# A new global order and engine choice for the operations ahead of the token mix, in a kernel of a gated long convolution followed by a gMLP mixer

## The chip, the cores and the metric

The kernel runs on one core of a Trainium2 chip. The core has five engines that each work through their own list of instructions in order: TensorE (PE, matrix products, with its weight loads listed apart as PEld), VectorE (DVE), ScalarE (ACT), GpSimd (POOL) and SyncE (SP, which issues most of the DMA transfers). They wait for one another by semaphores. The metric is device time in microseconds (us), the median of several executions. The profile is taken from one execution; its span runs from the first to the last instruction.

## The reference

Sequence length 2048 (16 tiles of 128 tokens), width 640 (5 blocks u of 128 channels), bf16. Cut to what matters:

```python
mod = (silu(c) @ w_mod).reshape(1, 6, 1, 640)
sa, ca, ga, sb, cb, gb = mod[:, 0], ..., mod[:, 5]

h = layernorm(q) * (1 + ca) + sa
k_shift = sum over t of k_pad[:, t:t + S] * shift_k[:, 3 - t]      # short convolution, 4 taps
kv = k_shift * v
y = irfft(rfft(kv, 2 S) * rfft(ssm_k, 2 S))[:S] + kv * ssm_D       # long convolution
x = q + ga * (h * y)

h = layernorm(x) * (1 + cb) + sb
z = gelu(h @ w_in)                                                # 640 -> 1728
z1, z2 = z[:, :864], layernorm(z[:, 864:])
g = w_sp @ z2 + b_sp[:, None]                                     # token mix, 2048 x 2048
return x + gb * ((z1 * g) @ w_out)
```

## The kernel before

The kernel is written as a plan. Each step of the computation is recorded as one of 1444 operations with the engines that may run it and the operations on which it depends. Nothing is scheduled by rule: a text constant named `ORDER` lists all operations, each as a letter for its engine (P for PE, D for DVE, A for ACT, G for POOL, S for SP) and its number. One loop hands them out in this order:

```python
        order = [(x[0], int(x[1:])) for x in ORDER.split()]
        assert sorted(i for _, i in order) == list(range(len(self.ops)))
        done = set()
        for e, i in order:
            o = self.ops[i]
            assert e in o["eng"] and done.issuperset(o["deps"]), (e, i)
            ...
            o["fn"](engines[e])
            done.add(i)
```

So `ORDER` fixes two things: the sequence on every engine, and which engine does an operation that has a choice. An engine that waits holds up everything behind it on its own list. Tiles lie in a fixed number of buffers per tag (four PSUM tags, `s1`, `sm`, `pu` and `pz`, serve everything up to the mix), and a new tile in a tag waits for the last reader of the tile that held the buffer.

The stages, with the names of operations that the text below uses (line numbers are of the kernel before):

- **Head and front** (0 to about 129 us). The long convolution is done as a Fourier transform by matrix products. Per block u of channels: the short convolution on PE and its product with v on DVE (L616), the first transform stage with its copies out of PSUM (`s1c`, 1024 columns in one copy or 512 in one, tile `s`, L278), the forward stage into `pu`, the product with the filter's spectrum (`prod`, L495, DVE alone, 1.2 us each, tiles `T` and `Tf` from `pu` and `KH`), for half of them a sum of halves (`csum`, L509, POOL or DVE), the inverse stage into `pz` and its copy out (`zc`, L278, tile `Z` from `pz`), then the last stage (`yl`, matrix products with `Ebd`) and the product with h (`ym`, L770). `zk` are the copies that regroup between stages. Beside it run the first layernorm (`xn`, L697 to L699, and `ghm`, L753, which applies 1 + ca and sa) and the sum x = q + ga * (...) (`res`, L808, with the statistics `ln2`, L814).
- **Second layernorm and zz** (about 125 to 191 us). The 16 tiles of tokens are taken in four groups of four. Per tile the aggregate, the power on POOL (L218 and L219), and the normalised tile (`zx`, L957 on ACT, L959 on POOL, L961 on DVE). The first group is transposed on PE in pieces (`hfl`, L972) and modulated by `hmod` (L983 on ACT, L985 on DVE). The other groups are transposed by one DMA each (L1003) and modulated in place, by channel block, by `hmod2` (five per group, L1009 on ACT, L1011 on DVE or POOL). Then come 64 groups of five matmuls of 432 columns (`zz`), each followed by a gelu on ACT (L1034) and, for the half that is normalised, a statistic (`stz`, L1040) and an aggregate (L1044). When four tiles have theirs, POOL makes the power (`rstdz`), DVE the offset (`nmrz`, L1049), and DVE or ACT normalise (`zn`, L1055 and L1057).
- **Token mix** (from 190.6 us). The product w_sp @ z2 is computed by seven products of halves (`m1` to `m7`), in the manner of Strassen's scheme, of sums of w_sp's blocks (`S1` to `S4`, L1101) and of z2's (`T1` to `T4`, L1111), at L1126. Then the output product.
- **Fill.** Four `fill` operations, each a few matmuls of the identity whose result nobody reads; the one that matters here, of two matmuls of 512 columns, stands ahead of the first zz.

## Time and profile before

| what | value |
|---|---|
| time, median of three runs | 305.8 us (305.66 to 307.07) |
| span of the profiled execution | 303.8 us |
| mean granted clock of TensorE in the span | 0.989 |
| instructions in the span | 7152 |
| bytes moved by DMA | 41.57 MB, 137 GB/s on average |

The profile gives no device time of the profiled execution itself; the 2.0 us between its span and the median are what lies around the span. PE does 2827 matmuls. A window view gives, for any stretch of the span, how long each engine was busy in it (with the number of instructions), the clock that TensorE was granted (1.00 is full speed), and the DMA engines' share. A group view gives one row per kind of instruction: line, engine, operation, output and input tiles with shapes, count, then busy time and mean duration in ns, then the idle time ahead of it. A timeline row is a start, a length, and what ran; neighbours of one kind are merged into one row with their count. The chain of waits is read backwards in time from the end: each piece is what the next one waited for.

### The profile page before, as it was taken

To read this page: it belongs to the slowest core of one execution; us is meant where nothing else is said; L and a number is where in the kernel's file an instruction comes from. 1 tells how busy PE (TensorE), PEld (TensorE's weight loads), DVE (VectorE), ACT (ScalarE), POOL (GpSimd) and SP (SyncE) were. 2 spreads that over 40 slices of the span, in tenths; PEclk is the share of its full clock that TensorE was granted. 3 is DMA by queue.
4 is the path that set the end of the run, shared out by engine and by line. 5 is a ranking of instruction groups with operands and counts; after the bars stand their busy time and mean duration, and the time that the engine had idled before them with its cause. 6 is when DMAs were issued, how large, how long until landed. Compare 5 with 4: busy or idle time off the path is not lost.

```text
span 303.8 us, 7152 instructions
## 1 busy us (share of the span) xinstructions
PE 293.1 (96%) x2827; PEld 207.0 (68%) x2827; DVE 260.4 (86%) x527; ACT 164.0 (54%) x299; POOL 186.8 (61%) x213
## 2 busy tenths in 40 slices
PE   6899999999999999799999999999999999999996
PEld 2788999999989988645555555555555555665664
DVE  8899999999989999989595988988678798886794
ACT  5989999998888865446665779500111102111110
POOL 5463788839769997577537342099531863476771
PEclk9999999999999999869999999999999999999999
DMA  7999869792397978005997900057654446452433
GB/s 143 270 242 271 194 177 282 134 223 39 77 186 163 287 122 276 2 2 105 157 234 154 197 0 4 0 117 150 132 133 90 102 112 141 102 84 73 91 83 121
DMA packets 117155, 41.57 MB, mean 137 GB/s; under 512 B 102557, under 2 KB 117122, under 8 KB 117122
## 3 DMA queue, kind: packets, MB, share of 16 engines
q1 hardware_dynamic: 116968, 41.08, 62.0%
q8 instruction: 22, 0.36, 0.5%
q14 instruction: 11, 0.09, 0.1%
q10 hardware_dynamic: 154, 0.05, 0.1%
HBM read 16.60 MB, written 2.63 MB: 63 GB/s over the span
## 4 chain that ended last, share of the span: by engine, by line
PE 80%; DVE 8%; SPq 5%; DMA 3%; issue 2%; POOL 1%; ACT 0%; DVEq 0%; POOLq 0%
PE ps L1126 23%; PE pu L275 19%; PE pz L275 17%; PE po L1335 5%; PE sm L275 5%; PE s L275 4%; SPq L570 3%; DVE Tf L495 3%; PE po L1348 3%; DMA ZT<-in_A_v_dram 3%; PE pz L1126 2%; PE pu L1126 1%; DVE Z L616 1%; SPq L585 1%; DVE ot L1394 1%
## 5 line engine op out<-in xcount | busy, mean ns | idle before, releaser
L275 PEld LDWEIGHTS <-Z 128*128 128x128 bf16 x320 | 32.0, 100 | 28.8 <-issue 3.0
L275 PE MATMUL pu<-X,M 128*128 128x128 bf16 (+1 forms) x480 | 45.6, 237 | 0.9 <-DVE Tf L495 0.7
L509 POOL TENSOR_TENSOR W<-Tf 128x256 bf16<-128x256 f32 x42 | 30.7, 745 | 15.0 <-DVE Tf L495 9.0
L275 PEld LDWEIGHTS <-M 128*128 128x128 bf16 x480 | 36.7, 98 | 4.2 <-issue 1.6
L1126 PEld LDWEIGHTS <-S 128*128 128x128 bf16 x256 | 25.0, 98 | 20.8
L275 PE MATMUL pu<-big,Z 128*128 128x432 bf16 x160 | 34.6, 360 | 0.0
L278 ACT CAST X<-s 128x1024 bf16<-128x1024 f32 x32 | 32.7, 1021 | 3.3 <-PE s L275 3.2
L275 PE MATMUL pz<-big,Z 128*128 128x432 bf16 x160 | 33.0, 349 | 0.0
L495 DVE TENSOR_TENSOR Tf<-pu,KH 128x1024 f32<-128x1024 f32 x25 | 30.3, 1215 | 1.2 <-ACT Z L278 0.5
L1132 ACT COPY m<-ps 128x432 f32<-128x432 f32 x7 | 3.6, 521 | 49.8 <-PE ps L1126 41.0
L1126 PEld LDWEIGHTS <-wT 128*128 128x128 bf16 x192 | 18.8, 98 | 15.3
L278 ACT CAST Z<-pz 128x512 bf16<-128x512 f32 x40 | 23.5, 596 | 4.9 <-PE pz L275 4.7
L275 PEld LDWEIGHTS <-G 128*128 128x128 bf16 x330 | 24.6, 98 | 1.8 <-issue 0.4
L278 ACT CAST KH<-pu 128x512 bf16<-128x512 f32 x40 | 23.1, 592 | 3.8 <-PE pu L275 3.4
L1126 PE MATMUL ps<-X,wT 128*128 128x432 bf16 x112 | 22.7, 346 | 0.0
L1126 PE MATMUL ps<-X,S 128*128 128x432 bf16 x112 | 22.6, 346 | 0.0
L1040 DVE BATCH_NORM_STATS2 stz<-X 128x6 f32<-128x432 bf16 x32 | 18.1, 588 | 5.0 <-ACT X L1034 4.9
L1126 PE MATMUL ps<-T,S 128*128 128x432 bf16 x112 | 22.2, 346 | 0.0
L275 PE MATMUL sm<-dg,big 128*128 128x128 bf16 x320 | 20.7, 219 | 1.1 <-DVE Z L616 1.0
L275 PEld LDWEIGHTS <-big 128*128 128x128 bf16 x320 | 18.9, 98 | 2.0 <-issue 1.6
L495 DVE TENSOR_TENSOR T<-pu,KH 128x1024 bf16<-128x1024 f32 x15 | 18.2, 1215 | 1.9 <-PE pu L275 1.8
L275 PEld LDWEIGHTS <-X 128*128 128x128 bf16 x288 | 17.8, 98 | 2.2 <-POOL X L433 0.7
(223 smaller groups left out, 666.7 us busy)
## 6 DMA issues: line engine op xcount, KB each, us to landing
wm<-in_w_mod_dram SPq DMA_DIRECT2D x6, 800.0 KB, 4.9
xt<-in_A_q_dram SPq DMA_DIRECT2D x4, 640.0 KB, 5.6
out_dram<-ot SPq DMA_DIRECT2D x15, 160.0 KB, 1.9
big<-in_B_w_in_dram SPq DMA_DIRECT2D x2, 1080.0 KB, 7.8
X<-in_A_ssm_k_dram SPq DMA_DIRECT2D x4, 512.0 KB, 6.2
ZT<-in_A_v_dram SPq DMA_DIRECT2D x1, 1024.0 KB, 7.6
big<-in_A_v_dram SPq DMA_DIRECT2D x1, 1024.0 KB, 7.8
w_o<-in_B_w_out_dram SPq DMA_DIRECT2D x6, 160.0 KB, 3.5
```

Source lines behind the costliest of these rows:

```text
L275: nc.tensor.matmul(o, lhsT=w, rhs=x, start=start, stop=stop)
L278: (e.copy if e is nc.scalar else e.tensor_copy)(dst, src)
L495: e.tensor_tensor(T_[:], (tl[pu] if src is None else tl[src])[:, :, :, None, :].to_broadcast(shape), tl[KH][:, :, None, :, :].to_broadcast ...
L509: e.tensor_tensor(tl[W][:, :, o, :], T_[:, :, 0, o, :], T_[:, :, 1, 1 - o, :], op=ALU.add if o else ALU.subtract)
L570: e.dma_start_transpose(k_of(u)[:, KPAD + h * m:KPAD + (h + 1) * m], A_k[0, h * m:(h + 1) * m, u * DU:(u + 1) * DU])
L585: e.dma_start(v_of(0, ns.start, NT // n) if u0 == 0 else tl[name][:], v_nat[:, ns, ds])
L616: e.tensor_tensor(dst, tl[ps][:].rearrange("p n (c g) -> p n c g", g=8), v_of(u, i * SCH, SCH).rearrange("p n (c g) -> p n c g", g=8), op= ...
L1040: op("D", "stz", lambda e, i=i, n=n, fc=fc: e.bn_stats(out=stz[:, n, fc, :], in_=tl[z2][:, i, fc * FC:(fc + 1) * FC]), r=[(z2, (i, fc))], ...
L1126: nc.tensor.matmul(ps[:, :FC], lhsT=lhs[:, s_, :], rhs=rhs(s_), start=(s_ == 0 and not more), stop=(s_ == HT - 1), skip_group_check=more)
L1132: e.copy(part[p, m][:], part[p, BANK[m]][:, :FC])
L1335: nc.tensor.matmul(ps[:, :HS], lhsT=w(k), rhs=x(k), start=start and k == 0, stop=stop and k == n - 1, skip_group_check=True)
L1348: e.matmul(po[t, i][:, :hi - lo], lhsT=uTs[t][:fsz[ft], ft, :], rhs=T["w_o"][:fsz[ft], ft, lo:hi], start=(ft == 0), stop=(ft == NFT - 1))
```

## The change

Only the constant `ORDER` differs. The first 1105 entries are put in another sequence, 107 operations are given to another engine, and the last 339 entries, from the middle of the token mix on, are the same as before. No operation is added or removed, so every engine's total changes only by what it takes over. The new constant has two more lines of text, so a line of code L985 in the kernel before is L987 in the changed one.

```diff
@@ ORDER (before: lines 48 to 111, after: lines 48 to 113) @@
-G5 D18 A1 S83 G0 G110 S2 P7 S23 G109 G6 D13 A4 D14 G25 A16 D15 D111 P1041 D10 S26 D112 P8 A38 D17 D113 A11 G89 D130
-A115 D136 P1044 S24 P153 S84 S91 A154 P156 P39 D131 P41 A158 A133 A132 S27 P1043 G90 D118 G134 D40 A137 D119 S3 A114
...
+D109 A4 D0 P1043 A1 G5 S23 P7 A10 A38 D13 D18 G110 D111 D118 D130 G15 G112 D119 A120 P1044 D131 A133 S83 D14 A16 P1041
+S2 G6 P8 A121 A11 A132 G25 P39 D136 A137 D113 A115 G17 D89 P153 A154 P156 A155 D124 D125 A127 A126 S84 S26 D40 D19
...
```

Of the operations that changed engine ahead of the first `hmod`, these go to DVE: from ACT five `zc`, five `s1c` and three or four single copies, from POOL eight `ghm`, three `csum`, two `res`, one `xn` and some small ones of the head. These leave DVE: ten `ghm`, five `csum`, two `xn` and a `res` for POOL, two `s1c` and three `zk` for ACT. On SP the loads keep their order but for one early pair.

Three places show it in rows. The first is on DVE, in the middle of the front. Before, around products of blocks 1 and 2 (tiles `T` and `Tf` out of `pu`; `gh` rows at L753 are `ghm`, rows at L770 `ym`):

```order
L616 TENSOR_TENSOR Z_1628<-sm_1788,big_1103 128x4x16x8
L495 TENSOR_TENSOR T_1876<-pu_1853,KH_1654 128x1024
L495 TENSOR_TENSOR Tf_1900<-pu_1879,KH_1619 128x1024
L753 TENSOR_TENSOR gh_95<-gh_95,gsa_bf_102 128x4x128
L753 TENSOR_TENSOR gh_95<-gh_95,gca1_bf_101 128x4x128 x2
L753 TENSOR_TENSOR gh_95<-gh_95,gsa_bf_102 128x4x128
L616 TENSOR_TENSOR Z_1628<-sm_1903,big_1103 128x4x16x8
L753 TENSOR_TENSOR gh_95<-gh_95,gca1_bf_101 128x4x128
L770 TENSOR_TENSOR gh_95<-gh_95,sm_1838 128x16x8x4
```

And in the changed kernel, around the products of the same stretch:

```order
L497 TENSOR_TENSOR Tf_1745<-pu_1738,KH_1434 128x1024
L497 TENSOR_TENSOR T_1764<-pu_1757,KH_1536 128x1024
L280 CAST Z_1346<-pz_1771 128x32x16
L280 CAST Z_1802<-pz_1803 128x32x16
L497 TENSOR_TENSOR T_1831<-pu_1824,KH_1602 128x1024
L280 CAST Z_1802<-pz_1833 128x32x16
L497 TENSOR_TENSOR Tf_1874<-pu_1867,KH_1657 128x1024
L772 TENSOR_TENSOR gh_95<-gh_95,sm_1748 128x16x8x4
L810 TENSOR_TENSOR xt_68<-xt_68,gh_95 128x4x128
```

Three copies `zc` (CAST of `Z` out of `pz`), which ACT made before, stand between four products, and the `ghm` that stood there have gone elsewhere.

The second is the start of zz. On PE, ahead of the first zz (`pu` out of `big` and `Z`), before:

```order
L972 MATMUL sm_2949<-ident_73,Z_2935 128x128
L275 LDWEIGHTS ident_73
L275 MATMUL s1_2969<-ident_73 128x512
L275 LDWEIGHTS ident_73
L275 MATMUL s1_2969<-ident_73 128x512
L275 LDWEIGHTS Z_2954
L275 MATMUL pu_2981<-big_2374,Z_2954 128x432
```

And now, at the end of the same transposes (`sm` out of the identity and `Z`; the rows `sm` out of `Ebd` are a `yl`, whose 32 matmuls reach up to the first zz):

```order
L974 MATMUL sm_2926<-ident_73,Z_2874 128x128
L974 LDWEIGHTS Z_2874
L974 MATMUL sm_2926<-ident_73,Z_2874 128x128
L277 LDWEIGHTS X_2716
L277 MATMUL sm_2935<-Ebd_100,X_2716 128x4x4
L277 LDWEIGHTS X_2716
L277 MATMUL sm_2935<-Ebd_100,X_2716 128x4x4
```

The fill (`s1` out of the identity) no longer stands there: it is now eight operations of PE's list ahead of zz, before the transposes. One `yl` stands between the transposes and zz instead. On DVE, the modulation of the second group of tiles (`hmod2`, in place on `Z`), before:

```order
L814 BN_STATS st2_72<-xt_68 128x6
L1011 TENSOR_SCALAR Z_3091<-Z_3091,cb1_col_70,sb_col_71 128x4x128
L814 BN_STATS st2_72<-xt_68 128x6
L1011 TENSOR_SCALAR Z_3091<-Z_3091,cb1_col_70,sb_col_71 128x4x128
L814 BN_STATS st2_72<-xt_68 128x6
L943 BN_AGGR mv2_82<-st2_72 128x2
L1040 BN_STATS stz_85<-X1_2980 128x6
L947 SCALAR_TENSOR_TENSOR nmr2_84<-mv2_82,rstd2_83 128x4
```

And now:

```order
L1042 BN_STATS stz_85<-X1_2997 128x6
L1013 TENSOR_SCALAR Z_3073<-Z_3073,cb1_col_70,sb_col_71 128x4x128
L945 BN_AGGR mv2_82<-st2_72 128x2
L1013 TENSOR_SCALAR Z_3073<-Z_3073,cb1_col_70,sb_col_71 128x4x128
L1042 BN_STATS stz_85<-X1_2997 128x6
L1046 BN_AGGR mvz_86<-stz_85 128x2
L1013 TENSOR_SCALAR Z_3073<-Z_3073,cb1_col_70,sb_col_71 128x4x128 x3
L816 BN_STATS st2_72<-xt_68 128x6 x6
```

Before, two of the group's five were DVE's, two POOL's and one ACT's; now all five are DVE's, with a statistic of zz (`stz`) ahead of them, and one more and two aggregates between them.

The third is on DVE at the fourth group of tiles. Before:

```order
L1040 BN_STATS stz_85<-X1_3207 128x6 x2
L1044 BN_AGGR mvz_86<-stz_85 128x2
L1040 BN_STATS stz_85<-X1_3378 128x6 x2
L1044 BN_AGGR mvz_86<-stz_85 128x2
L1011 TENSOR_SCALAR Z_3418<-Z_3418,cb1_col_70,sb_col_71 128x4x128 x2
L1040 BN_STATS stz_85<-X1_3378 128x6
L1011 TENSOR_SCALAR Z_3418<-Z_3418,cb1_col_70,sb_col_71 128x4x128
L1040 BN_STATS stz_85<-X1_3207 128x6
```

And now:

```order
L1042 BN_STATS stz_85<-X1_3332 128x6
L1013 TENSOR_SCALAR Z_3431<-Z_3431,cb1_col_70,sb_col_71 128x4x128
L1046 BN_AGGR mvz_86<-stz_85 128x2
L1042 BN_STATS stz_85<-X1_3194 128x6
L1046 BN_AGGR mvz_86<-stz_85 128x2
L1013 TENSOR_SCALAR Z_3431<-Z_3431,cb1_col_70,sb_col_71 128x4x128
L1046 BN_AGGR mvz_86<-stz_85 128x2
L1042 BN_STATS stz_85<-X1_3332 128x6
L1013 TENSOR_SCALAR Z_3431<-Z_3431,cb1_col_70,sb_col_71 128x4x128
```

Before, the first two of DVE's three modulations stood together; now a statistic and two aggregates stand between them, and the last one still stands behind a statistic of its own. The other two of the five were POOL's; now they are one POOL's and one ACT's.

At the end of zz one zz group moves from ahead of the products to behind `m4`, and `m6` becomes the third product.

## The prediction

> **What bounds the kernel now.** I read the profile from the whole to the place: first the busy times and the chain that ended last, then the span cut into stages, then the waits inside the stage that the change rearranges.

> ```profile
> PE 293.1 (96%) x2827; PEld 207.0 (68%) x2827; DVE 260.4 (86%) x527; ACT 164.0 (54%) x299; POOL 186.8 (61%) x213
> PE 80%; DVE 8%; SPq 5%; DMA 3%; issue 2%; POOL 1%; ACT 0%; DVEq 0%; POOLq 0%
> ```

> TensorE (PE) is busy for 96% of the span and carries 80% of the chain. No matmul is added or removed, so the change can only win or lose PE's idle time, 303.8 - 293.1 = 10.7 us, and time in which PE runs at a lower clock. Where both lie is seen by stage (columns: window, its length, then busy time of PE, weight load, DVE, ACT, POOL, then granted clock, DMA share, GB/s):

> ```profile
> 0.00:24.40 24.40, 20.75 (x237) 16.44 (x238) 21.09 (x64) 20.22 (x44) 13.24 (x35) 1.00 1.08 214
> 24.40:60.00 35.60, 35.26 (x548) 33.21 (x545) 33.71 (x61) 34.60 (x66) 25.02 (x34) 1.00 0.90 218
> 60.00:100.00 40.00, 39.73 (x569) 36.86 (x568) 37.90 (x57) 34.49 (x53) 29.82 (x34) 1.00 0.69 138
> 100.00:128.69 28.69, 25.24 (x490) 23.54 (x487) 27.07 (x52) 18.13 (x32) 23.31 (x27) 0.97 0.62 173
> 128.69:190.77 62.08, 62.08 (x333) 32.90 (x334) 51.21 (x149) 41.28 (x77) 32.27 (x36) 0.96 0.53 104
> 190.77:303.80 113.03, 110.06 (x661) 64.02 (x659) 89.38 (x148) 15.27 (x32) 63.12 (x50) 1.00 0.47 103
> ```

> The first four rows are the convolution with its ends, the fifth the 64 groups zz, the sixth the products and the mix. PE idles 3.65 us up to 24.4, 0.34 and 0.27 in the two middle rows, 3.45 from 100 to 128.69, and not at all in the fifth row, where the clock of 0.96 shows that some of it was slow. So PE bounds from 24.4 to 100 and through zz. But **DVE stands right behind it**: its idle time in the first four rows is 3.31 + 1.89 + 2.10 + 1.62 = 8.92 of 128.69 us, which is 93% busy. What is written on DVE there must fit in 8.92 us.

> The head ends with a transfer that both orders issue at nearly the same place on SP's queue. I therefore count no gain there. The last 3.45 us of PE's idle time are a chain through small operations:

> ```profile
> 125.88 0.88 POOL Z L959
> 126.81 0.69 PE s L972 x6
> 127.58 1.06 DVE Z L985 x3
> 128.69 1.03 PE s L275 x2
> 129.72 1.44 PE pu L275 x4
> ```

> Normalise (Z L959), transpose (hfl, L972), modulate (hmod, L985), then the fill's two matmuls (s L275), then zz (pu L275). This is what the first zz waits for.

> **The change, part by part. DVE up to the start of zz.** Of 107 engine changes those that count are the ones onto and off the fullest vector engine. The prices, grouped by line and shape up to 129 us (last columns: count, busy us, mean ns):

> ```profile
> L509 DVE TENSOR_TENSOR W<-Tf 128x256 bf16<-128x256 f32 x8 | 3.4, 433 | 0.2
> L753 DVE TENSOR_TENSOR gh<-gh,gca_bf 128x512 bf16<-128x512 bf16 x11 | 4.4, 437 | 0.0
> L753 DVE TENSOR_TENSOR gh<-gh,gsa_bf 128x512 bf16<-128x512 bf16 x10 | 5.1, 510 | 0.0
> L278 DVE CAST X<-pu 128x512 bf16<-128x512 f32 x3 | 2.0, 681 | 0.0
> L278 DVE COPY X<-sm 128x1024 bf16<-128x1024 bf16 x6 | 4.0, 668 | 0.1
> L699 DVE TENSOR_SCALAR gh<-xt,mv,rstd 128x640 bf16<-128x640 bf16 x2 | 1.4, 688 | 0.0
> L808 DVE TENSOR_TENSOR xt<-xt,gh 128x512 bf16<-128x512 bf16 x4 | 2.8, 699 | 0.0
> ```

> Onto DVE, ahead of the first hmod, come five copies zc and five copies s1c from ACT, each a 128x512 cast out of PSUM: 10 x 0.681 = 6.8. Eight ghm at the mean of 0.437 and 0.510, 0.47: 3.8. Three csum at 0.433: 1.3. Two res at 0.699: 1.4. One xn at 0.688 and two bf16 copies at 0.668: 2.0. About eight small operations (masks, identity, diagonal) from POOL and ACT, which DVE does not show: at nothing they are 0, at the 0.433 of the nearest row 3.5; as most are narrower, I take 2.3. Sum 17.6. Off DVE go ten ghm, 4.7; five csum, 2.2; two xn, 1.4; one res, 0.7; three copies zk and two s1c, five at about 0.67, 3.4; small ones, taken at 1.1 between 0 and 3. Sum 13.5. **DVE gets about 4.1 us more work**, 2 to 6 with the small ones at their ends. ACT loses about as much, and POOL gains a little under 2; both have over 20 us idle in the four rows, though ACT, 34.60 of 35.60, has only 1.0 in the second.

> What 4.1 us do is decided by the 8.92. If DVE uses 4.1 of them, 46%, PE stays the bound and the front ends when it did: 0. If none can be used, it ends 4.1 later. If DVE keeps up with less waiting than that, what can be won is PE's idle 3.45 before 128.69, and no more. The waits on which it hangs are of two kinds:

> ```profile
> DVE T L495 <- PE pu L275: 1.8, 4, 0.8
> DVE Z L616 <- DMA ZT<-in_A_v_dram: 0.5, 1, 0.5
> DVE Tf L495 <- ACT Z L278: 0.5, 1, 0.5
> ```

> These are DVE's longest waits from 24.4 to 117. Most are a product waiting for its transform, four times for 1.8 in total: time into which an independent copy fits exactly. The wait on ACT's copy (0.5) goes where DVE makes the copy itself. I take the front at **0**, between -3.4 and +4.1. Against it speaks that a DVE copy now stands between two products in the row: the products queued behind it (1.2 us each, and PE's inverse transform behind them) wait for its PSUM tile. With PE nearly gapless, each such wait comes out of PE's time unless another inverse is in hand.

> **The start of zz.** The fill leaves its place between hmod and zz.

> ```profile
> 128.00 1.02 ACT L983 ACTIVATE Z<-sm,sb_col,cb_col 128x256 bf16<-128x256 bf16 x2 [1.33 <-PE sm L972]
> 129.51 3.81 PE L275 MATMUL pu<-big,Z 128*128 128x432 bf16 x10
> ```

> DVE's hmod end at 128.64 and ACT's at 129.02; zz, which began at 129.51, could begin then: -0.49. One yl now stands behind hfl and fills a part of PE's pause ahead of zz. The clock, in windows of 3.4 us, and the matmuls that it slowed:

> ```profile
> 123.60:127.00 3.40, 1.97 (x75) 1.87 (x73) 2.96 (x14) 0.92 (x1) 2.13 (x4) 1.00 0.02 5
> 127.00:130.40 3.40, 2.62 (x15) 1.38 (x13) 3.40 (x10) 1.02 (x2) 2.46 (x4) 0.50 0.00 0
> 130.40:133.80 3.40, 3.40 (x11) 1.37 (x9) 3.40 (x13) 1.35 (x2) 3.28 (x4) 0.50 0.00 0
> ```
> ```profile
> 133.11 2.35 PE L275 MATMUL pz<-big,Z 128*128 128x432 bf16 x10
> 135.30 0.50 PE L972 MATMUL s<-ident,Z 128*128 128x128 bf16 x6
> 144.07 1.99 PE L275 MATMUL pu<-big,Z 128*128 128x432 bf16 x10
> 145.89 1.81 PE L275 MATMUL pz<-big,Z 128*128 128x432 bf16 x9
> ```

> After a window in which PE was busy for 1.97 of 3.40 us the granted clock was 0.50 for two windows. Ten zz matmuls then took 133.11 - 129.51 = 3.60, and the next ten 2.19, where ten at full clock take 145.89 - 144.07 = 1.82: a loss of 1.78 + 0.37 = 2.15 (the next ten begin at 133.11 and end ahead of the transposes at 135.30). The changed order moves the pauses, but its tail chain is as long, so whether the clock falls again I hold at one in two.

> [...]

> [...]

> ```profile
> 138.88 3.00 SPq L1003 DMA_TRANSPOSE Z<-Z  x1
> 143.86 0.43 DVE L1011 TENSOR_SCALAR Z<-Z,cb_col,sb_col 128x512 bf16<-128x512 bf16 x1
> 144.41 0.58 DVE L1011 TENSOR_SCALAR Z<-Z,cb_col,sb_col 128x512 bf16<-128x512 bf16 x1
> 145.11 0.81 ACT L1009 ACTIVATE Z<-Z,sb_col,cb_col 128x512 bf16<-128x512 bf16 x1
> ```

> Its first zz follows the five matmuls at 145.89, at 146.81, 0.89 after the last hmod2 (145.92). With fill and clock gone PE would be there at 146.81 - 0.49 - 2.15 = 144.2. In the new order all five hmod2 stand on DVE, a statistic of zz ahead, and another with two aggregates between: 5 x 0.5 and about 1.3 (two statistics of 0.54, the row further down, and 0.2) are 3.8. They begin between the landing (141.87, or 141.4 with the fill gone) and the old 143.86, so they end between 145.2 and 147.7. Thus the gain is at most 146.81 - 145.2 = 1.6, and it can be a loss of 0.9. I take **-0.8**, near the favourable end, as DVE's wait there was for a gelu that comes earlier too.

> **The rest of zz and the mix.** Group 3's first zz needs a hmod2 that now queues on DVE behind a statistic waiting for its gelu:

> ```profile
> 169.82 0.53 ACT L1034 ACTIVATE G<-pz 128x432 bf16<-128x432 f32 x1 [0.87 <-PE pz L275]
> 170.30 0.39 DVE L1011 TENSOR_SCALAR Z<-Z,cb_col,sb_col 128x512 bf16<-128x512 bf16 x1
> 170.53 1.99 PE L275 MATMUL pu<-big,Z 128*128 128x432 bf16 x10
> 170.61 1.62 DVE L1040 BATCH_NORM_STATS2 stz<-X 128x6 f32<-128x432 bf16 x3
> ```

> Group 3 begins with the second five at 170.53, at 171.44; its last modulation ended at 170.69, 0.75 before. A statistic is 1.62 / 3 = 0.54 and the gelu ahead of it 0.53; if the modulation comes later by both, 1.1, it uses up the 0.75 and PE waits **+0.4**, between 0 and +1. At the end of zz T2 is wanted one product earlier (m6 third). Its second half follows rstdz by nmrz, four zn and one sum, and is read after m6's fourth matmul; I cost it at 0, up to +0.9 (the length of one zz group, which stood ahead of the products and now follows m4). The last 339 operations keep their order: 0.

> Sum: 0 - 0.8 + 0.4 = -0.4. The profiled span is 303.8 and the median 305.8, so 2.0 lie around the span; I keep them: 303.4 + 2.0 = **305.4**.

> **The rivals.** *Faster:* DVE's idle time takes the 4.1 its products end earlier, and PE work that stood before 100 is left to fill the last chain's pause. For it: 1.8 us of its waits are for PE, and PE has 3.45 idle there. Against: DVE would be near 98% busy. At two thirds of the 3.45, -2.3, with z's -0.8 and group 3's +0.4 it is 303.1. It is over 0.5% once PE's 3.45 shrinks by more than 1.1. *Slower:* DVE becomes the bound of the products. Only the idle time of 24.4 to 100, 3.99, is near the new copies; if half of it is usable, 2.0, the front ends 4.1 - 2.0 = 2.1 later and the time is 307.5, and with none 309.5. For it: 93% busy before, and copies that stand ahead of products. It costs over 0.5% as soon as DVE absorbs less than 4.1 - 1.9 = 2.2. *No effect on the front, and z gated:* hmod2 on DVE ends as late as before; the start of zz gives nothing: 306.2. *The clock falls later,* and both windows, 6.8 us, lie wholly in zz: 3.4 lost for the 2.15 of now, so 305.8 + 1.25 - 0.49 + 0.4 = 307.0; for it, the pauses shift against windows that the kernel doesn't set. *The clock does not fall:* the start of zz gives its full 1.6 where the hmod2 allow it, 305.8 - 1.6 + 0.4 = 304.6; for it, the pause that the yl fills; against it, that 1.97 us of matmuls did not keep the clock up before. [...]

> **How the numbers follow.** About 0.5%, 1.5 us, is what can be told from no change here. The forecast, the front at 0, has 0.38 and its own range of 304.3 to 307.3, whatever zz does: of the 0.38, the half gain has 0.17, clock kept 0.10, gated 0.06, clock later 0.05, which lie between 304.6 and 307.0. Faster has 0.36, slower 0.26. The range is 302.4 to 308.4: below it about a quarter of the faster case, above it about two fifths of the slower one.

> **What would show it.** DVE's idle time before the first zz: about 4.8 if the first step is right, about 7 or more where DVE is late. First zz near 129.0. The clock at 0.5 for two windows or for none. Group 1's first zz between 145.5 and 147. A pause under 1 us ahead of group 3. Wrong it would be if PE pauses inside 24.4 to 100, or if the last chain's pause shrinks by more than 1.1.

## The result

The changed kernel takes 327.69 us (median of 4 runs, 324.53 to 329.81) beside 305.73 (305.32 to 307.07): **1.0625** times as long, 95% interval 1.0574 to 1.0675. Two of its four runs fell into the slower state, which the ratio leaves out; without them it is about 325. The forecast was 305.4.

The page of the changed kernel, its busy times and the chain that ended last:

```profile
PE 297.7 (92%) x2827; PEld 207.9 (64%) x2827; DVE 280.5 (87%) x546; ACT 155.9 (48%) x287; POOL 186.4 (57%) x206
PE 49%; DVE 35%; DMA 4%; ACT 4%; POOL 3%; issue 3%; DVEq 0%; POOLq 0%; SPq 0%
```

DVE is busy 20 us longer than before (280.5 for 260.4), and its share of the chain has gone from 8% to 35%: it has taken PE's place as the bound over long stretches. Where the 20.3 us of span (303.8 to 324.1) went is read from windows, cut at the changed kernel's first zz and its first product (columns as in the prediction):

```profile
0.00:24.40 24.40, 20.45 (x224) 15.52 (x225) 22.31 (x63) 19.02 (x39) 15.84 (x35) 1.00 1.02 211
24.40:60.00 35.60, 34.68 (x530) 32.12 (x528) 34.24 (x66) 35.10 (x69) 25.41 (x33) 1.00 1.06 220
60.00:100.00 40.00, 38.89 (x553) 36.41 (x551) 38.35 (x54) 31.22 (x47) 34.26 (x37) 1.00 0.59 124
100.00:133.42 33.42, 28.50 (x537) 26.47 (x536) 31.95 (x59) 17.81 (x33) 22.80 (x28) 0.94 0.64 165
133.42:202.22 68.80, 62.08 (x331) 32.22 (x328) 54.24 (x150) 38.04 (x73) 23.57 (x24) 0.96 0.46 94
202.22:324.10 121.88, 113.14 (x667) 65.14 (x666) 99.38 (x161) 14.68 (x31) 64.50 (x52) 0.99 0.44 96
```

The front ends 3.91 later (133.42 for 129.51). The zz stage, without a gap before, now has 68.80 for 62.08 of work. The waits of PE between 130 and 250 us (what waited, for whom: total, times, longest) are a list that has no row at all before:

```profile
PE pu L277 <- DVE Z L1013: 3.4, 3, 2.3
PE ps L1128 <- DVE c L1157: 3.0, 1, 3.0
PE pu L1128 <- DVE T L1113: 2.8, 1, 2.8
PE pz L277 <- DVE Z L1013: 2.3, 1, 2.3
PE s L974 <- POOL Z L961: 1.1, 1, 1.1
PE pz L277 <- ACT Z L1011: 0.6, 1, 0.6
PE pz L277 <- ACT M L1036: 0.5, 1, 0.5
```

With the starts of the same work in both timelines the loss adds up, in order: front 3.9; zz 8.6 (the second group 2.3, the third 2.4, the fourth 3.9, each later than the one ahead of it by so much; the third's are 1.7 of halved clock and a wait of 0.6 for ACT's modulation); m6 behind T2 3.0; the mix behind DVE 3.1; and 1.7 because the products behind that wait ran slowly. That is 20.3. (m5 starts only 11.6 late for 12.5 of delay, as one zz group, 0.91, has been moved behind m4.)

What the prediction did not have is in the durations. The timeline of DVE and POOL from 97 to 103 us and from 144 to 148 us (start, length, engine, operation, count):

```profile
97.13 2.58 DVE L755 TENSOR_TENSOR gh<-gh,gsa_bf 128x512 bf16<-128x512 bf16 x3
100.76 0.92 DVE L755 TENSOR_TENSOR gh<-gh,gsa_bf 128x512 bf16<-128x512 bf16 x1
101.60 1.37 DVE L810 TENSOR_TENSOR xt<-xt,gh 128x512 bf16<-128x512 bf16 x1
...
98.09 1.33 POOL L810 TENSOR_TENSOR xt<-xt,gh 128x512 bf16<-128x512 bf16 x1
100.25 2.44 POOL L755 TENSOR_TENSOR gh<-gh,gsa_bf 128x512 bf16<-128x512 bf16 x2
...
144.00 1.41 DVE L963 TENSOR_SCALAR Z<-xt,mv,rstd 128x640 bf16<-128x640 bf16 x1
145.34 1.37 DVE L810 TENSOR_TENSOR xt<-xt,gh 128x512 bf16<-128x512 bf16 x1
146.95 1.05 DVE L810 TENSOR_TENSOR xt<-xt,gh 128x512 bf16<-128x512 bf16 x1
...
144.08 3.64 POOL L810 TENSOR_TENSOR xt<-xt,gh 128x512 bf16<-128x512 bf16 x3
```

POOL's last one ends at 147.72, DVE's last one at 148.00. In these rows all of DVE's operations but the first, at 97.13, take 0.9 to 1.4 us, and each ends 0.2 to 0.3 us behind one of POOL's. The trace of before holds the plainest case, which the prediction passed over:

```profile
161.37 2.75 POOL L1203 TENSOR_TENSOR w_o<-w_o,gb_bf 128x640 bf16<-128x640 bf16 x2
161.43 1.35 DVE L1049 SCALAR_TENSOR_TENSOR nmrz<-mvz,rstdz 128x4 f32<-128x4 f32 x1
```

An operation on four columns, which takes 0.16 at 205.88 in the changed kernel, lasts 1.35 and ends at 162.78, when the first of POOL's two is through (162.76). Such a **collision** is DVE standing still while POOL works, and it counts as busy time.

### The profile page after: what moved, and what is told of

Its sections match the earlier page's. It is cut to its first block, busy times and chain, and to the rows that moved or that the text cites. A ratio compares the mean times of both kernels' runs of the same rounds, so it can differ in the third digit from the quotient of the medians.

```text
span 324.1 us, 7152 instructions
## 1 busy us (share of the span) xinstructions
PE 297.7 (92%) x2827; PEld 207.9 (64%) x2827; DVE 280.5 (87%) x546; ACT 155.9 (48%) x287; POOL 186.4 (57%) x206
## 4 chain that ended last, share of the span: by engine, by line
PE 49%; DVE 35%; DMA 4%; ACT 4%; POOL 3%; issue 3%; DVEq 0%; POOLq 0%; SPq 0%
PE ps L1128 19%; PE pz L277 7%; PE pu L277 7%; PE po L1337 5%; DVE stz L1042 4%; PE sm L277 4%; DVE st L816 3%; DVE xt L810 3%; DMA ZT<-Z 3%; PE po L1350 2%; DVE w_o L1205 2%; DVE T L497 2%; DVE Tf L497 2%; DVE X L1059 2%; PE s L277 2%
## 5 line engine op out<-in xcount | busy, mean ns | idle before, releaser
L277 PE MATMUL pu<-X,M 128*128 128x128 bf16 (+1 forms) x480 | 46.3, 237 | 4.5 <-DVE T L497 3.1
L511 POOL TENSOR_TENSOR W<-Tf 128x256 bf16<-128x256 f32 x44 | 32.9, 764 | 15.5 <-DVE Tf L497 13.2
L277 PE MATMUL pz<-big,Z 128*128 128x432 bf16 x160 | 35.3, 365 | 3.3 <-DVE Z L1013 2.3
L277 PE MATMUL pu<-big,Z 128*128 128x432 bf16 x160 | 33.1, 347 | 3.4 <-DVE Z L1013 3.4
L280 ACT CAST Z<-pz 128x512 bf16<-128x512 f32 x35 | 20.5, 597 | 8.4 <-PE pz L277 8.3
L220 POOL TENSOR_SCALAR rstd<-mv 128x4 f32<-128x4 f32 (+2 forms) x7 | 1.5, 209 | 30.1 <-DVE mv L945 27.9
```

Of the source, the lines that this page charges most:

```text
L277: nc.tensor.matmul(o, lhsT=w, rhs=x, start=start, stop=stop)
L280: (e.copy if e is nc.scalar else e.tensor_copy)(dst, src)
L511: e.tensor_tensor(tl[W][:, :, o, :], T_[:, :, 0, o, :], T_[:, :, 1, 1 - o, :], op=ALU.add if o else ALU.subtract)
```

## The experiments

Theory A: the loss is several causes, each in its own stage. Theory B: all of it follows from the front. Theory C: collisions make DVE late. Theory D: DVE simply has more work. Further ones (A1, A2, E, G) are told where they are used. Unless another interval is given, each ratio is to the kernel before on the same chip. Most kernels change entries of `ORDER` only.

**e1 and e2: the two halves.** The list is cut at the first zz.

```diff
 e1: changed kernel's entries up to its first zz, then before's order and engines
 e2: before's entries up to its first zz, then the changed order and engines
```

> The new order and engines up to the first zz, then the old order and engines. Theory A (the loss has separate causes, each in its own stage): first zz near 133.4 as in the changed kernel (+3.9), no long pause of PE behind it, time 309 to 313. Theory B (everything behind the front is late only because DVE comes out of the front late): the pauses at the second to fourth group and in the mix are there too, time 320 or more.

> The old order and engines up to the first zz, then the new ones. Theory A: first zz at 129.5 as before, then the pauses of the changed kernel at the fourth group, at m6 (2.8) and in the mix (3.0 and a slower clock): time 315 to 322. Theory B: within 2 of the kernel before, 304 to 308.

e1 took 310.69 (ratio 1.0164, 1.0138 to 1.0190) with its first zz at 132.94; e2 took 323.90 (1.0582, 1.0538 to 1.0627). Theory A holds and B falls: 5.1 and 18.3 us apart, with the same waits at the fourth group, at m6 and in the mix in e2 as in the changed kernel. e1 is in its band, e2 2 us above it. The two add up to 23.4, more than the changed kernel's 19, in part because the clock in e2 stands at 0.5 for four windows from 124.84 on instead of two.

**e3 and e4: sequence or engines.**

```diff
 e3: changed sequence, each letter as before      (107 letters back)
 e4: before's sequence, each letter as changed    (107 letters)
```

> The new sequence with every operation on the engine that it had before. Theory A1 (the engine choice does the harm: more work on DVE, and DVE and POOL hold each other up when both read SBUF): time 304 to 312. Theory A2 (the sequence does the harm: operations of zz and of the normalisation queue behind others that wait): 315 or more.

> The old sequence with every operation on its new engine. Theory A1: 315 or more, with first zz at 133 or later. Theory A2: 305 to 311, about the 4.1 us more work on DVE at most.

358.15 (1.1715, 1.1672 to 1.1757) and 332.86 (1.0903, 1.0838 to 1.0967). e3 lies in the band of A2 and e4 in that of A1, which exclude each other, so neither theory holds: both halves alone are worse than both together, e3 far worse. A sequence is fitted to its engines, so a letter changed back does not measure that letter. The same shows in **e8 and e14**, which take back part of the engine choice in e1:

```diff
 e8, in e1:  -D224 D286 D302 D346 D382   (zc)   +A224 A286 A302 A346 A382
 e14, in e1: the 45 letters of the front exchanged between D and G as before
```

> e1_new_front (new front, old rest, 310.7) with the five zc copies back on ACT. Theory E (the front is late by the work added to DVE): 3.4 us less on DVE, first zz 2.5 to 3.5 earlier, time 307 to 308.5. Rival (the front is late by the sequence or by collisions): 310 to 311.

> e1_new_front (310.7) in which the 45 operations of the front that changed between DVE and POOL have their old engine again, in the new sequence; those that changed between DVE and ACT keep the new one. Theory C (collisions between DVE and POOL carry most of the front's 3.9 us): 307 to 308.5. Theory G (the sequence was fitted to its engines, and any part of the choice taken back costs): 312 or more, as e8 did with the copies zc.

312.58 (1.0218, 1.0191 to 1.0245) and 322.04 (1.0510, 1.0464 to 1.0557). Both miss theories C and E; e14 lies in G's band. In e8 3.4 us less work on DVE made the kernel 1.9 slower: a product on DVE now waits 1.9 for a copy on ACT (0.5 in e1), and PE's waits for products `Tf` grow from 0.5 to 1.7. These two decide nothing about collisions.

**e5: collisions at the second group.** Five operations of POOL go to DVE, which gives DVE more to do.

```diff
-G720 G677 G620 G653 G706
+D720 D677 D620 D653 D706
```

> The changed kernel with five operations between 134 and 148 us (one ghm and four res) moved from POOL to DVE, in the same sequence. Theory C (a DVE operation with two inputs in SBUF, and a DVE normalisation, does not start while POOL reads SBUF: five DVE operations there took 1.05 to 1.42 where the same shapes take 0.36 to 0.44 alone): DVE does five operations more (about 2.0 us) and still comes through earlier, because 4.7 us of collisions go; the DMA that transposes group 2 is issued 2 to 3 us earlier than at 145.5, time 322 to 325. Theory D (DVE simply has too much work): group 2 starts 1 to 2 us later, time 327 to 329.

324.53 (1.0610, 1.0580 to 1.0641). The timeline of DVE in e5 at the same operations, and one normalisation:

```profile
134.48 0.76 DVE L810 TENSOR_TENSOR xt<-xt,gh 128x512 bf16<-128x512 bf16 x2
143.54 0.44 DVE L963 TENSOR_SCALAR Z<-xt,mv,rstd 128x640 bf16<-128x640 bf16 x1
145.41 0.41 DVE L810 TENSOR_TENSOR xt<-xt,gh 128x512 bf16<-128x512 bf16 x1
146.26 0.74 DVE L810 TENSOR_TENSOR xt<-xt,gh 128x512 bf16<-128x512 bf16 x2
```

Every one is back at 0.36 to 0.44. DVE does five operations more and is through sooner: the transposing DMA of the second group is issued at 144.08 for 145.51, its first zz starts at 151.03 for 153.00, the fourth group at 180.96 for 184.31. Theory C holds here and D falls, though the DMA gained 1.4 and not 2 to 3. Of the 3.35 us only 1.5 are left in the span (322.6 for 324.1): the clock fell at the fourth group and behind m6's wait instead, and the mix waited for DVE all the same. In time e5 (324.2 to 325.1) can't be told from the changed kernel at its about 325.

**e6 and e12: the fourth group first.** DVE's modulations (hmod2) are written ahead of statistics that wait for their gelu; e6 also moves the group's DMA.

```diff
 e6:  +S985 A987 behind D984, D986 D988 D989 ahead of D951, G990 ahead of G837
 e12: +D986 D988 D989 G990 G837 D838 D941 behind S985 (S985 stays)
```

> The changed kernel with the fourth group's transposing DMA and its five modulations written directly behind the normalisation, ahead of statistics and of the power rstdz. Theory A: PE's pauses at the fourth group (2.26 + 0.57 + 0.55) go, first zz of the fourth group 3 to 4 us earlier than at 184.3 to 186.7, time 321.5 to 323. Rival (the time is only handed on to the next wait, m6): within 1 of the changed kernel.

e6 took 336.80 (1.1005, 1.0969 to 1.1041). On SP's queue the transposing DMA now stood ahead of two loads of w_sp and waited there for its input, and a sum on DVE that needs those loads waited for them, with the modulations behind it:

```profile
185.49 0.69 DVE L1103 TENSOR_TENSOR S<-wT 128x1024 bf16<-128x1024 bf16 x1 [10.42 <-DMA wT<-in_B_w_sp_dram]
```

The edit did more than it was meant to: a DMA moved on SP's queue displaces the loads that it passes.

> The changed kernel with DVE's three modulations of the fourth group and POOL's one written directly behind the group's transposing DMA, whose own place among the loads on SP's queue is kept. In e6 it was moved past two loads of w_sp, and DVE waited 10.4 us for them. Theory A: the pauses of the fourth group (3.4 in all) shrink to under 1, its zz are done 2.5 to 3.5 us earlier, and time is 322 to 324 if m6's wait stays the same. Rival (handed on): m6's wait grows by as much, 325 or more.

e12 took 324.66 (1.0616, 1.0588 to 1.0644), no different from the changed kernel. Its waits of PE between 128 and 250 us:

```profile
PE ps L1128 <- DVE c L1157: 2.9, 1, 2.9
PE pu L1128 <- DVE T L1113: 2.9, 1, 2.9
PE pz L277 <- DVE Z L1013: 2.3, 1, 2.3
PE pu L277 <- ACT G L1036: 1.9, 1, 1.9
PE pz L1128 <- DVE T L1113: 1.1, 1, 1.1
```

The 3.4 us in three waits for the fourth group's modulation are gone, as theory A has it, and 1.9 behind a gelu and 1.1 behind T have come ahead of the products: nearly all was handed on, though m6's own wait did not grow, as the rival had it. The row was a wait, but not the bound.

**e7 and e16: the mix.** e7 moves the scaling of w_out back into zz; e16 leaves it on DVE and takes POOL's sums away from beside it.

```diff
 e7:  -S1052 D1056 D1055 D1057 D1053 D1059 D1054 in the mix
 e7:  +S1052 behind S919; +G1056 G1055 G1057 G1053 behind G979; +D1059 D1054 behind D989
 e16: -G1067 G1108 G1113
 e16: +D1067 D1108 D1113
```

> The changed kernel with the scaling of w_out (gbm) taken out of the mix: its load and six of its seven operations go back into the zz stage, four of them to POOL. Theory A: PE's wait of 2.96 for DVE in the mix and the two slow-clock windows behind it (about 1.7) go, time 320.5 to 322. Rival (gbm on POOL collides with DVE in zz, or the wait has another cause): 324 or more.

> The changed kernel with three sums of w_sp's blocks (ssum at 215, 221 and 223 us) moved from POOL to DVE, in the same sequence. Beside them DVE's scalings of w_out took 1.4 to 2.4 instead of 0.47 and one product 2.28 instead of 0.6. Theory C: DVE does 2.0 us more, loses 4 to 6 us of collisions, PE's wait of 2.96 in the mix goes and with it the slow clock behind it, time 320.5 to 322.5. Theory D (DVE's load): the wait grows by 2, 327 or more.

The scaling on DVE (L1205) in the changed kernel:

```profile
215.69 3.71 DVE L1205 TENSOR_TENSOR w_o<-w_o,gb_bf 128x640 bf16<-128x640 bf16 x2
219.90 0.72 DVE L1205 TENSOR_TENSOR w_o<-w_o,gb_bf 128x640 bf16<-128x640 bf16 x1
223.87 3.20 DVE L1205 TENSOR_TENSOR w_o<-w_o,gb_bf 128x640 bf16<-128x640 bf16 x3
```

And in e16:

```profile
218.34 1.69 DVE L1205 TENSOR_TENSOR w_o<-w_o,gb_bf 128x640 bf16<-128x640 bf16 x2
221.13 0.48 DVE L1205 TENSOR_TENSOR w_o<-w_o,gb_bf 128x640 bf16<-128x640 bf16 x1
223.77 1.28 DVE L1205 TENSOR_TENSOR w_o<-w_o,gb_bf 128x640 bf16<-128x640 bf16 x3
```

The same six operations take 3.45 for 7.63, while DVE does three sums more. PE's wait in the mix is gone: from m5 to the first output product it is 26.97 (203.11 to 230.08) for 30.59. So the mix's wait is collisions, not load. e7, with the scaling gone from there, shows the same 26.97. In total both fell short: e16 has 323.78 (1.0585, 1.0539 to 1.0631; span 321.4), e7 326.83 (1.0697, 1.0652 to 1.0742). In e16 the clock fell at the fourth group and behind m6's wait instead. In e7 the fourth group's zz waits 6.8 for its modulation, where the longest of three waits was 2.3, and the rival holds: the four scalings on POOL meet the normalisation of that group on DVE:

```profile
171.14 1.35 DVE L949 SCALAR_TENSOR_TENSOR nmr<-mv,rstd 128x4 f32<-128x4 f32 x1 [1.40 <-POOL rstd L221]
172.41 4.83 DVE L963 TENSOR_SCALAR Z<-xt,mv,rstd 128x640 bf16<-128x640 bf16 x4
171.07 5.62 POOL L1205 TENSOR_TENSOR w_o<-w_o,gb_bf 128x640 bf16<-128x640 bf16 x4
```

In the changed kernel the same five operations of DVE take 0.16 and 1.51. So the group's transposing DMA is issued at 177.31 for 174.89, although DVE came to the normalisation 2.1 earlier.

**e9, e17 and e18: what bounds the new front.** e9 moves four operations from POOL to DVE in e1. e17 and e18 move nothing: they leave an operation's instructions out.

```diff
 e9:       -G622 G643 G680 G686
 e9:       +D622 D643 D680 D686
 e17, e18: -            o["fn"](engines[e])
 e17, e18: +            if i not in SKIP:
 e17, e18: +                o["fn"](engines[e])
```

> e1_new_front (310.7) with four operations of the front (three ghm and one res, around 85 to 103 us) moved from POOL to DVE, in the same sequence. They are the ones beside which DVE operations of that stretch took 0.9 to 1.4 instead of 0.4. Theory C (collisions): DVE does 1.6 us more and loses 3.4 us of collisions, first zz 1 to 2 us earlier than at 132.9, time 308.5 to 309.7. Theory D (DVE's load): first zz 1.6 later, 312 or more.

> e1_new_front (310.7, first zz 132.9) with the seven ghm of the front that came from POOL to DVE left out of the computation (4.0 us of DVE's time between 68 and 99); all else stays as and where it is. If DVE is the bound of the new front: first zz 2.5 to 4 us earlier, time 307 to 308.5. If PE waits for something else there: within 1 of 310.7.

> e1_new_front with POOL's 24 operations ghm and res of the front left out of the computation (29.3 us of POOL's time between 66 and 127); DVE's own list is untouched. Theory C (DVE loses 4 us or more of the front to collisions with POOL): DVE comes through 60 to 122 us 2 to 4 us sooner with the same work, first zz as much earlier, time 307 to 309. Theory D (only DVE's own work counts): first zz within 1 of 132.9, 310 to 311.

e9 took 311.03 (1.0167, 1.0142 to 1.0191), outside both bands. Four operations more made the last product of the front only 0.4 later (120.31), but one of them (1.37 at 85.64) met the next of POOL's in its turn, so the collision moved on. e17 took 308.82 (1.0088, 1.0068 to 1.0108), and e18 308.53 (1.0081, 1.0065 to 1.0097), for e1's 310.69. The first zz moved by less than was expected, 1.4 and 1.7 us; e17 lies between its two bands, e18 in that of theory C by its time alone. The last product of the front starts at 115.42 before, 119.92 in e1, 118.07 in e17 and 117.81 in e18. Windows of e1 and e18 from 60 to 104 us:

```profile
60.00:104.00 44.00, 40.96 (x594) 38.35 (x592) 42.37 (x57) 34.30 (x52) 37.81 (x40) 1.00 0.61 125
```

```profile
60.00:104.00 44.00, 42.99 (x619) 40.23 (x617) 41.40 (x61) 34.22 (x53) 14.88 (x22) 1.00 0.65 124
```

In e18 DVE's list is the same, and it gets through 61 operations in 41.40 us of busy time where it took 42.37 for 57; PE gains 2.0. So the front's loss at the last product, 4.5, is in part work (1.9 of it goes with seven ghm, whose 4.0 us are 7 x 0.41 of work and some 1.1 of collisions) and in part collisions with those 24 operations (2.1). In e18 POOL's other sums may also come earlier, so the 2.1 is an upper end. What the remaining half-microsecond is, and whether the two add, was not tried.

**e10, e11 and e13: the kernel before, with the fill moved.**

```diff
 e10: -P1042 behind the transposes P773 P774   +P1042 ahead of P773
 e11: e10, and P751 (yl) behind P774
 e13: e10, and -D618 +G618 (the res that took 1.42)
```

> The kernel before with nothing changed but the fill, which moves from between the modulation and the first zz to ahead of the transposes. My prediction's step: first zz 0.49 earlier, time 305.0 to 305.5 with the clock falling as before, 303.5 to 304.5 if the matmuls of the fill, now ahead of the pause, keep the clock up. Rival (the second group's modulation gates it): no change, 305.5 to 306.

> As e10, and the last yl moves behind the two transposes, so that it fills PE's pause ahead of the first zz, as in the changed kernel. If the pause is what lowers the clock: clock 1.00 throughout and 303.5 to 304.5. If DVE needs that yl earlier: first zz unchanged or later, 305.5 to 307.

> e10 (the kernel before with the fill moved ahead of the transposes, 304.0), and the one res of the front that took 1.42 on DVE beside POOL's ghm goes to POOL. Theory C: 1.4 us off DVE, which stands right behind PE, first zz up to 1 us earlier, 303 to 304. Theory G: POOL's sums come later and a product waits for them, 304.5 or more.

e10: **304.04, ratio 0.9940 (0.9920 to 0.9961)**; e11: 304.39 (0.9954, 0.9937 to 0.9972); e13: 303.83 (0.9944, 0.9926 to 0.9962). PE in e10 at the same place:

```profile
125.12 0.83 PE L277 MATMUL s<-ident 128*128 128x512 bf16 x2
126.56 0.82 PE L974 MATMUL s<-ident,Z 128*128 128x128 bf16 x6 [0.60 <-POOL Z L961]
127.94 3.78 PE L277 MATMUL pu<-big,Z 128*128 128x432 bf16 x10
```

The first zz is 1.57 earlier (127.94 for 129.51), and the span 1.6 shorter: all of it reaches the end. The clock fell for two windows in all three kernels, in e11 too, with a yl in the pause behind the transposes. So e10 and e11 lie in the bands for a clock that stays up without that being the reason; in e11 the first zz is at 128.98, 1.0 later than in e10. e13 and e10 can't be told apart, so e13 shows no gain from one collision less. One entry of the changed order, taken alone, thus gives a kernel 0.6% faster than the one before, with an interval that excludes 1.

## Why the prediction was wrong

Term by term, the front at 0, the start of zz at -0.8, the rest of zz at +0.4, its end at 0 and the mix at 0 came out as 3.9, 2.3, 6.3, 3.0 and 4.8: together 20.3 us.

**The front: "I take the front at 0".** This step failed, by 3.9 us, and in both of its terms. In the new front DVE is idle for 2.09 + 1.36 + 1.65 + 1.47 = 6.57 us, so up to the first zz at 133.42 it is busy for 126.85. Before, with 8.92 of idle time up to 129.51, it was 120.59. That is 6.3 more where I had 4.1. And of the 8.92 only 2.35 could be used, not 4.1: the quarter, not the half. Of the 2.2 that were missing in the work, 1.9 can be counted as collisions: from 24.4 on DVE's ghm, res, csum and xn take 4.9 us longer than the same shapes alone in the changed kernel, and 3.0 before. I priced res at the 0.699 mean of a row whose members ran from 0.41 to 1.42; a mean that mixes free and colliding operations is the price of neither. PE then waited for a product (`T`, 3.1 us in four waits, and `Tf`, 0.5; before 0.7 in two), the rival called slower by its mechanism. Its price, 2.1 to 4.1, holds the 3.9, but in part by luck: more work was added than it has, and more of it absorbed than at its upper end. e1's 310.7 with the new front alone stands near its 309.5.

**The start of zz: "-0.8".** The fill's -0.49 was under-sized: e10 shows -1.57. I let zz wait for the last modulation, ACT's. In e10 that one ends at 128.91, and zz has begun at 127.94; before, the fill stood behind DVE's last one (128.64) and itself ran on the halved clock. The gate that I put behind it, the second group of four tiles at 145.2 at the earliest where its first zz stood at 146.81, was worked out for the changed order's modulations, which e10 does not have; there group two begins at 145.18. In the changed kernel the gate did hold, and worse than my +0.9: +2.3 on top of the front, because the normalisation that feeds the transposing DMA was late, in part by five collisions (e5: 2.0 of it). I had counted DVE's modulations, but not what stands on DVE ahead of the DMA that they wait for.

**The clock: one in two.** It fell, at 129.34 for two windows, and again for one window at 153.23 and at 228.32. In the changed kernel the 2.30 us of waiting ahead of 153.00 were enough for the second fall:

```profile
149.60:153.00 3.40, 1.10 (x7) 0.39 (x5) 3.37 (x12) 1.06 (x2) 0.00 (x0) 1.00 0.95 127
153.00:156.40 3.40, 3.40 (x11) 1.39 (x12) 3.37 (x14) 0.00 (x0) 0.19 (x1) 0.53 0.18 41
```

In these windows of the changed kernel PE is busy for 1.10 of 3.40, and the clock of the next is 0.53. Such a wait thus cost over half as much again behind it (1.7 behind these 2.3 and behind the mix's 3.0). The wait of m6, 2.8, cost only itself: the clock's windows cut it in two at 207.85, and the clock stayed at 1.00. My sum gave every wait only its own length.

**The rest of zz: "+0.4".** The mechanism was found and its size missed: the fourth group loses 3.9, and the third 2.4, for which I had no term (1.7 of it is the halved clock). I compared one statistic and one gelu with 0.75 of slack; in the trace nine statistics and nmrz, which waits for POOL, stand on DVE between 178.2 and the first of the modulations at 183.9. But e12 shows that the place was not the bound: without that wait the time is the same.

**The end of zz: "at 0, up to +0.9".** m6 waited 2.82. The chain through the power on POOL, nmrz, four zn and a sum was named, and its length not added up. No run shortened it; that it is the bound there is read from the trace alone. The timeline of DVE in the changed kernel:

```profile
203.57 0.21 DVE L1046 BATCH_NORM_AGGREGATE mvz<-stz 128x2 f32<-128x12 f32 x1
203.69 1.01 DVE L1113 TENSOR_TENSOR T<-X,T 128x1728 bf16<-128x1728 bf16 x1
205.88 0.16 DVE L1051 SCALAR_TENSOR_TENSOR nmrz<-mvz,rstdz 128x4 f32<-128x4 f32 x1 [1.18 <-POOL rstdz L221]
205.96 1.74 DVE L1059 TENSOR_SCALAR X<-X,mvz,rstdz 128x864 bf16<-128x864 bf16 x4
207.74 2.03 DVE L1113 TENSOR_TENSOR T<-X,T 128x1728 bf16<-128x1728 bf16 x2
```

From the aggregate's end at 203.78 to the first sum's end, half of the last row, at 208.76 it is 5.0 us, and m6 was ready for it 2.8 earlier.

**"The last 339 operations keep their order: 0."** True, but the entries ahead of them, up to the first output product, are in the mix too, and there I looked only at the products: six scalings of w_out now stand there, on DVE, beside POOL's sums. In e16, without most of their collisions, all of the 4.8 us that the mix loses (the wait and the slow clock) are gone; it gains only 3.6 there, as it has a slow clock behind m6 that the changed kernel does not have.

The chances: slower had 0.26, with a price up to 309.5 for the time. Every rival was one mechanism in one stage; none was the sum of several stages that lose in the same way.

## What to carry to other kernels

Where DVE and POOL work side by side, price a DVE operation with two SBUF inputs by whether POOL is at work beside it (0.4 or 1.4 here), not by a mean; work moved to DVE can be slower than where it came from, and taking POOL's work over too can make DVE faster (e5, e16), while giving DVE's work to POOL can make DVE slower (e7). A sequence and its engine choice are one thing: change one letter in it and new waits appear, so test a cause by leaving work out or by moving both partners. And a wait removed is worth what the next one leaves: ask for it in every stage up to the end, DMA queues included.

## What the hardware showed

Where a DVE operation is held up beside one of POOL's, it is not slowed in proportion: it ends just behind POOL's. It took 1.37 for 0.41 on 128x512 (from 135.81 in the changed kernel: POOL's sum is through at 136.89, DVE's at 137.18), 1.41 for 0.44 on a normalisation of 128x640 (from 144.00) and 1.35 for 0.16 on 128x4 (from 161.43 before). How long it stands goes by POOL's operation and not by its own: a scaling that takes 0.47 alone took 2.40 beside a sum of 2.57 on POOL (from 215.69 and from 215.18 in the changed kernel). It can fall on POOL as well: beside a csum and two ghm of DVE, 0.41 each from 68.20 in the changed kernel, a ghm on POOL took 2.09 (from 68.20 too), where the shortest of its kind there take 1.15. Products out of PSUM (`T` and `Tf` from `pu`) show none of it: in the two traces the 76 beside POOL take 1.20 to 1.23, the four without it 1.21 to 1.22. Nor do the statistics of zz, 0.55 to 0.61 both for the 27 beside POOL and for the 37 without.
